# Doing segment 1's layer norm in the opening of a fused attention and GLU kernel

## The chip, the cores and the metric

The kernel runs on one core of a Trainium2 chip. The metric is device time in microseconds (us), the median of a few executions; a lower time is better. The engines are called as the profile calls them: PE is TensorE (PEld its weight loads), DVE is VectorE, ACT is ScalarE, POOL is GpSimd, and SP is SyncE, whose queue issues nearly all transfers here.

## The reference

One adaptive-norm block with segmented attention, followed by a bilinear GLU. All arrays are float32, there are 2048 tokens of width 512, 32 heads of 16, and 4 segments of 512 tokens.

```python
h = _layernorm(x) * (1 + ca) + sa            # norm of every token, scaled and shifted per column
for s in range(4):                           # segments of 512 tokens, q/k/v of h
    logits = q_s @ k_s.T * scale + mask      # causal inside the segment
    a_dot  = softmax(logits) @ v_s
    a_mem  = (phi(q_s) @ M) / (phi(q_s) @ z + 1e-6)      # memory of the earlier segments
    o_s    = g * a_mem + (1 - g) * a_dot
    M, z   = M + phi(k_s).T @ v_s, z + sum(phi(k_s))     # phi(t) = t + 1 if t > 0 else exp(t)
x = x + ga * (o @ wo)
x = x + gb * ((h2 @ w_gate) * (h2 @ w_up) @ w_down)      # h2: second norm, with cb and sb
```

The vectors sa, ca, ga, sb, cb and gb come from `silu(c) @ w_mod`.

## The kernel before

**Attention part.** A segment's norm (`ln`, through `a_ln`) reads four tiles of x (128 tokens by 512). For each tile VectorE takes statistics (a bn_stats and a bn_aggr). Then two ACT instructions (Ln, Exp) and a few four-element operations, on VectorE for segment 0 and on POOL for the others, give 1/sqrt(var+eps). Four tensor_scalar instructions on VectorE normalise the tiles. After that the tiles are transposed on PE and scaled, shifted and split in two parts (`ahH`, `ahL`) by ACT and POOL. Keys and queries are made per group g of 8 heads (`a_kq`): 12 matmuls into a PSUM bank (`kps`, `qps`), a copy `kf`/`qf` on ACT, and a split in three bfloat16 parts, for groups 1 to 3 with ACT and POOL (`k`, `kr` on lines 823 to 828 for keys, the same for queries). They are written to DRAM (`kd`, `qd`) and read back in a different layout as `kst` and `qst`. The features phi of the keys are made by ACT and finished by a scalar_tensor_tensor on VectorE (`phk`).

**The loop over units.** A unit is half a group: four heads of one segment. For each there are passes of PE: `q` tiles (queries by keys), whose row maxima VectorE takes straight from PSUM in a custom instruction (line 39, out `q`, and the maxima in `nm`), and `k` tiles (keys by queries), whose exponentials ACT writes to `pt`. The q tiles live in two PSUM banks, `lq0` and `lq1`, used in turn: PE can write the next q tile into a bank only after VectorE is through with the one before. Between these tiles PE gets other work ("fill"): keys, queries and values of later groups and segments, memories, the output projection. Before the loop stands the opening: modulation vectors, segment 0's norm, keys and queries of groups 0 and 1, and `gates`, which makes `omg` and `gg` from beta with a few VectorE instructions, copies `omg` into eight value tiles on POOL (line 683) and scales the head mask `hmg` with both.

**What sets the order.** PE's instructions are chained in program order by `pe`. `CV` and `CA` chain the VectorE and ACT instructions issued through them in the same way; instructions issued through `vec` or `act` join that chain only when those are switched to it, which is done for `vec` just before the loop (`vec.eng = CV`). The rest is placed by a list scheduler at build time, so each engine has a fixed order at run time. Before the change, segment 1's norm is woven into segment 0's groups 2 and 3 inside the loop, nine steps in all: four pairs of statistics, the small operations, four normalisations. Its x goes into the four buffers `x`, which before that hold segment 0's x and then the raw weights `wk` and `wq` of groups 1 and 2 (the list `stage`).

Of the kernel before, what the change touches and what calls it, by code (L numbers as in the profile page):

```python
# [8 lines left out]
F32 = mybir.dt.float32  # L9
F32R = mybir.dt.float32r  # L10
BF = mybir.dt.bfloat16
AF = mybir.ActivationFunctionType
# [5 lines left out]
P = 128  # L18
# [39 lines left out]
def tile_kernel(ctx, tc, x, wq, wk_, wv, wo, beta, w_gate, w_up, w_down, c, w_mod, out):  # L58
# [113 lines left out]
    def ln(pool, hpool, xt, s, sc, sh, pfx, hb, fast):  # L172

        first = pfx == "a" and s == 0
        V, A = (CV, CA) if first else (vec, act)
        mv = pool.tile([P, 4, 2], F32, tag="mv", name=f"{pfx}mv{s}", bufs=2)
        for t in range(4):
            st = pool.tile([P, 6], F32, tag="st", name=f"{pfx}st{s}_{t}", bufs=2)
            i = V.bn_stats(st, xt[t])
            if not first:  # L180
                pin(i)
            V.bn_aggr(mv[:, t, :], st)
            if not first:
                yield 0.0
        sd = pool.tile([P, 4], F32, tag="sd", name=f"{pfx}sd{s}", bufs=2)
        A.activation(sd, mv[:, :, 1], AF.Ln, bias=epst[:, 0:1])
        y = pool.tile([P, 4], F32, tag="y", name=f"{pfx}y{s}", bufs=2)
        A.activation(y, sd, AF.Exp, scale=-0.5)
        a = pool.tile([P, 4], F32, tag="ya", name=f"{pfx}ya{s}", bufs=2)
        b = pool.tile([P, 4], F32, tag="yb", name=f"{pfx}yb{s}", bufs=2)  # L190
        eng = CV if first else nc.gpsimd
        eng.tensor_mul(a, y, y)
        if first:
            CV.scalar_tensor_tensor(b, mv[:, :, 1], EPS, a, op0=ALU.add, op1=ALU.mult)
        else:
            eng.tensor_scalar(b, mv[:, :, 1], 1.0, EPS, op0=ALU.mult, op1=ALU.add)
            eng.tensor_mul(b, b, a)
        eng.tensor_scalar(b, b, -0.5, 1.5, op0=ALU.mult, op1=ALU.add)
        eng.tensor_mul(y, y, b)
        yield 0.0  # L200
        tps = [bank(f"{pfx}tp{s}_{d}") for d in range(KT)] if first else []
        for t in range(4):
            i = V.tensor_scalar(xt[t], xt[t], mv[:, t, 0:1], y[:, t:t + 1],
                                op0=ALU.subtract, op1=ALU.mult)
            if not first:
                pin(i)
                yield 0.0
            for d, ps in enumerate(tps):
                TP(ps[:, t * P:(t + 1) * P], xt[t][:, d * P:(d + 1) * P], ident)
        if first:  # L210
            yield 0.0
        hH, hL = [], []
        if first:
            hcur[0] = hH, hL
        for d in range(KT):
            if first:
                ps = tps[d]
            else:
                ps = bank(f"{pfx}tp{s}_{d}", small=pfx == "c" and s == 0)
                for t in range(4):  # L220
                    TP(ps[:, t * P:(t + 1) * P], xt[t][:, d * P:(d + 1) * P], ident)
            h = pool.tile([P, L], F32, tag="hf", name=f"{pfx}hf{s}_{d}", bufs=hb[2])
            A.activation(h, ps, AF.Identity, scale=sc[:, d:d + 1], bias=sh[:, d:d + 1])
            hi = hpool.tile([P, L], F32R, tag=hb[0].format(d), name=f"{pfx}hH{s}_{d}", bufs=hb[1])
            lo = hpool.tile([P, L], F32R, tag=hb[0].format(4 + d), name=f"{pfx}hL{s}_{d}", bufs=hb[1])
            if fast:
                if d % 2:
                    A.activation(hi, h, AF.Copy)
                else:
                    V.tensor_copy(hi, h)  # L230
                V.tensor_sub(lo, h, hi.bitcast(F32))
            else:
                act.activation(hi, h, AF.Copy)
                nc.gpsimd.tensor_sub(lo, h, hi.bitcast(F32))
            hH.append(hi)
            hL.append(lo)
            yield 0.45
            if pfx == "a" and not first and d % 2 == 1:
                yield False
        return hH, hL  # L240
# [500 lines left out]
                i += 1  # L741

    wH, wL = {}, {}
    stage = [("ph", 3), ("ph", 3), ("ph", 3), ("mem", 1), ("pkr", 1), ("f", 2)] + [("x", 4)] * 4 + [("mem", 1), ("memb", 2)]
    nst = [0]

    def staged(nm):
        tg, n = stage[nst[0] % len(stage)]
        nst[0] += 1
        return (ap if tg == "memb" else pa).tile([P, D], F32, tag=tg, name=f"wr{nm}", bufs=n)  # L750

    def load_g(nm, w, g):
# [46 lines left out]
    def a_kq(s, g, nm):  # L799

        hH, hL = hcur[0]
        ph = phs.setdefault((s, g), {})
        if True:
            dst = kd if nm == "k" else qd
            ps = bank(f"{nm}ps{s}_{g}")
            n = 0
            three = ((wH, hH), (wH, hL), (wL, hH)) if s == 0 and g < 2 else ((wH, hH), (wL, hH), (wH, hL))
            terms = [(k, *ab) for k in range(KT) for ab in three]
            if s == 0 and g == 1:
                terms.sort(key=lambda t: t[1] is wL)  # L810
            for k, a, b in terms:
                MM(ps, a[nm, g][:, k, :], b[k], start=n == 0, stop=n == 11)
                n += 1
                if n in (3, 6, 9):
                    yield 0.68
            f = pa.tile([P, L], F32, tag="f", name=f"{nm}f{s}_{g}", bufs=2)
            fast = s == 0 and g == 0
            A, V = (CA, CV) if fast else (act, nc.gpsimd)
            A.activation(f, ps, AF.Copy)
            q3 = pa.tile([P, 3, L], BF, tag="q3", name=f"{nm}3_{s}_{g}", bufs=2)  # L820
            r = pa.tile([P, L], F32, tag="qr", name=f"{nm}r_{s}_{g}", bufs=2)
            i0, i1, i2 = (0, 1, 2) if nm == "k" else (2, 1, 0)
            A.activation(q3[:, i0, :], f, AF.Copy)
            V.tensor_sub(r, f, q3[:, i0, :])

            def rest():
                (CV.tensor_copy if fast else act.copy)(q3[:, i1, :], r)
                V.tensor_sub(q3[:, i2, :], r, q3[:, i1, :])
                nc.sync.dma_start(dst[s][g].rearrange("r p t -> p r t"), q3)

            if fast:
                rest()
            phi = (nm == "k" and s < NSEG - 1) or (nm == "q" and s > 0)
            if phi:
                if fast:
                    yield 0.0
                if nm == "q" and g > 0:
                    yield from drain()
                e = pa.tile([P, L], F32, tag="ph", name=f"ph{nm}{s}_{g}", bufs=3)
                if behind or after:  # L840
                    settle()
                rl = pa.tile([P, L], F32, tag="rl", name=f"rl{nm}{s}_{g}", bufs=1)
                ph[nm] = e

                def feature():
                    for a, fn in ((rl, AF.Relu), (e, AF.Exp)):
                        i = (CA if fast else act).activation(a, f, fn)
                        if lastex[0] is not None:
                            tc.add_manual_dep(i.ins, lastex[0].ins.name, NOSYNC, reason="order")

                def feature2():
                    pin((CV if fast else vec).scalar_tensor_tensor(e, e, 1.0, rl, op0=ALU.min, op1=ALU.add))

                held = s > 0 or g > 1
                if held:
                    behind.append(lambda: (feature(), after.append(feature2)))
                else:
                    feature()
            yield 0.68
            if not fast:  # L860
                rest()
            if phi and not held:
                later.append(feature2)
                if fast:
                    flush()
        nkq[s, g] = nkq.get((s, g), 0) + 1
        if nkq[s, g] == 2:
            done.add((s, g))
# [107 lines left out]
    def fill_a():  # L976
# [1 line left out]
            next(w)  # L978
        yield from av
        memq.extend((a_mem(0, 0), a_mem(0, 1)))  # L980
        lns = None
        for s in range(NSEG):
            if s > 0:
                hcur[0] = yield from lns
# [2 lines left out]
            for g in range(2 if s == 0 else 0, NG):  # L987
# [5 lines left out]
                K, Q = a_kq(s, g, "k"), a_kq(s, g, "q")  # L993
                if s == NSEG - 1 and g == 0:
                    B["orl"] = wo_load(0, wpool)
                if g >= 2 and s + 1 < NSEG:
                    if g == 2:
                        xts[s + 1] = xload(s + 1)
                        lns = a_ln(s + 1)
                        Q = weave(Q, lns, (0, 1, 2, 3))  # L1000
                    else:
                        K = weave(K, lns, (1,) if s > 0 else (0, 1, 3))
                        Q = weave(Q, lns, (0, 1, 2, 3) if s > 0 else (0, 1))
                if g == 1 and 0 < s < 3:
                    acc = mod_acc(r)
                    K, Q = weave(K, acc, (0, 2)), weave(Q, acc, (0, 2))
# [120 lines left out]
    w1 = [load_g(nm, w, 1) for nm, w in (("k", wk_), ("q", wq))]  # L1127
    for w in w1:
        next(w)
    run(kq0[1])  # L1130
    run(kq0[0])
    load(0)
# [4 lines left out]
        next(w)  # L1137
    for i in range(3):
        next(av)
    gates()  # L1140
    w2 = [load_g(nm, w, 2) for nm, w in (("k", wk_), ("q", wq))]
    for w in w2:
# [536 lines left out]
```

## Time and profile before

| | |
|---|---|
| median of 3 runs | 854.42 us (854.02 to 854.63) |
| the profiled execution's own time | 853.83 us |
| span of the profiled execution | 852.1 us |
| PE busy | 835.4 us (98%) |
| DVE busy | 641.9 us (75%) |
| ACT busy | 498.0 us (58%) |
| POOL busy | 275.7 us (32%) |

The span runs from the first to the last instruction; 1.7 us of the execution's own time lie around it. Timeline rows give the start in the span, the duration in us, the engine, the line, the operation with output and inputs, the count of merged instructions, and in brackets the idle time of the engine just before with what ended it. Window rows give busy time and count of each engine in a stretch of time.

### The profile page before, as it was taken

The numbers are of one execution on the slowest core, as the hardware profiler recorded it, in microseconds if no ns is written. First come the engines' busy times: TensorE is split into PE (matmuls) and PEld (weight loads), VectorE is DVE, ScalarE is ACT, GpSimd is POOL, SyncE is SP. The second block draws the span as 40 slices with busy tenths as digits, with TensorE's granted clock in tenths as the row PEclk, the third lists the DMA queues.
The fourth block names the chain that finished last, engine by engine and source line by source line (L and its number), as shares of the span: only waits on it lengthen the run. The fifth ranks groups of instructions, "written<-read, shape, count | busy, mean of one in ns | idle before, by whom it ended". The sixth has DMA issues, their size and how long they took to land.

```text
span 852.1 us, 14420 instructions
## 1 busy us (share of the span) xinstructions
PE 835.4 (98%) x4982; PEld 598.2 (70%) x4982; DVE 641.9 (75%) x1796; ACT 498.0 (58%) x759; POOL 275.7 (32%) x423
## 2 busy tenths in 40 slices
PE   9989999999999999999999999999999999999998
PEld 6756656666665656656665687887888778888886
DVE  7897868887778967787888359989987855447654
ACT  4758767787676876677545626344435546455230
POOL 2756627566565774675424610000000000000000
PEclk9999999999999999999999999999999999999999
DMA  9655445564545554457675457587650675335102
GB/s 272 153 150 158 111 114 136 164 171 120 144 103 166 146 163 106 123 155 230 173 233 161 137 193 238 187 286 273 233 220 28 234 269 211 123 135 185 42 9 98
DMA packets 83928, 139.57 MB, mean 164 GB/s; under 512 B 12720, under 2 KB 46768, under 8 KB 83856
## 3 DMA queue, kind: packets, MB, share of 16 engines
q1 hardware_dynamic: 83568, 138.52, 52.6%
q8 instruction: 39, 0.64, 0.3%
q14 instruction: 33, 0.27, 0.1%
q10 hardware_dynamic: 288, 0.15, 0.1%
HBM read 89.87 MB, written 48.50 MB: 162 GB/s over the span
## 4 chain that ended last, share of the span: by engine, by line
PE 60%; DVE 4%; ACT 2%; POOL 2%; issue 1%; DMA 0%; DVEq 0%; POOLq 0%; ACTq 0%
PE acc L1355 14%; PE Xu L1286 7%; PE Xg L1286 7%; PE wops L85 5%; PE tb L85 4%; PE Yu L1286 4%; PE Yg L1286 4%; PE k L85 3%; PE q L85 3%; DVE q L39 2%; PE Zg L1286 1%; PE Zu L1286 1%; PE qps L85 1%; PE vps L85 1%; PE ctp L88 1%; PE Xx L1286 1%
## 5 line engine op out<-in xcount | busy, mean ns | idle before, releaser
L39 DVE CUSTOM_DVE_ANT_0 q<-q,cmask 128x384 f32<-128x384 f32 (+3 forms) x512 | 248.3, 503 | 72.2 <-PE q L85 64.6
L335 ACT ACTIVATE pt<-k 128x1024 f32<-128x1024 f32 x160 | 163.9, 1024 | 74.2 <-PE k L85 72.2
L341 POOL TENSOR_SCALAR_AFFINE_SELECT pt<-pt 128x256 f32<-128x256 f32 (+1 forms) x224 | 97.6, 449 | 137.9 <-ACT pt L335 135.9
L85 PE MATMUL q<-kst,qst 96*128 96x384 bf16 (+3 forms) x512 | 122.8, 302 | 6.4 <-DVE nm L39 5.1
L85 PE MATMUL k<-qst,kst 98*128 98x384 bf16 (+3 forms) x512 | 96.0, 299 | 1.6 <-ACT pt L335 1.3
L1363 DVE TENSOR_TENSOR xa<-xa,acc 128x512 f32<-128x512 f32 x95 | 64.9, 684 | 39.1 <-PE acc L1355 38.5
L85 PEld LDWEIGHTS <-qst 96*128 96x128 bf16 x512 | 43.9, 98 | 57.8 <-issue 43.0
L85 PE MATMUL tb<-pt,v 128*32 128x512 f32 (+3 forms) x1024 | 75.7, 436 | 0.3 <-POOL pt L341 0.3
L39 DVE DVE_READ_ACCUMULATOR2_ANT nm<- 128x1 f32 x512 | 72.0, 141 | 0.0
L85 PEld LDWEIGHTS <-kst 98*128 98x128 bf16 x512 | 44.5, 98 | 25.0 <-issue 8.8
L1355 PE MATMUL acc<-dH,mH 128*128 128x512 f32 (+1 forms) x152 | 60.3, 397 | 0.0
L1355 PE MATMUL acc<-dL,mH 128*128 128x512 f32 (+1 forms) x152 | 60.1, 395 | 0.0
L1355 PE MATMUL acc<-dH,mL 128*128 128x512 f32 (+1 forms) x152 | 60.0, 395 | 0.0
L85 PEld LDWEIGHTS tb<-pt,v 128*32 128x32 f32 x1024 | 28.6, 109 | 39.2 <-issue 35.5
L367 ACT ACTIVATE tsb<-tb 128x512 f32<-128x512 f32 x32 | 19.1, 596 | 31.7 <-PE tb L85 31.6
L1355 PEld LDWEIGHTS acc<-dL,mH 128*128 128x128 f32 (+1 forms) x152 | 28.6, 188 | 7.1
L1355 PEld LDWEIGHTS acc<-dH,mL 128*128 128x128 f32 (+1 forms) x152 | 28.5, 188 | 7.1 <-DVE mL L1306 0.3
L1355 PEld LDWEIGHTS acc<-dH,mH 128*128 128x128 f32 (+1 forms) x152 | 28.5, 188 | 6.7
L85 PE MATMUL kps<-ahH,wkH 128*128 128x512 f32 x64 | 29.5, 460 | 0.0
L85 PE MATMUL qps<-ahH,wqH 128*128 128x512 f32 x64 | 28.7, 449 | 0.0
L85 PE MATMUL wops<-woH,oH 128*128 128x512 f32 x64 | 28.3, 442 | 0.0
L85 PE MATMUL vps<-wvH,ahH 128*128 128x512 f32 x64 | 28.3, 442 | 0.0
(399 smaller groups left out, 2018.4 us busy)
## 6 DMA issues: line engine op xcount, KB each, us to landing
wm<-in_w_mod_dram SPq DMA_DIRECT2D x24, 256.0 KB, 4.6
kd<-k SPq DMA_DIRECT2D x16, 384.0 KB, 2.5
qd<-q SPq DMA_DIRECT2D x16, 384.0 KB, 3.3
kst<-kd SPq DMA_DIRECT2D x32, 192.0 KB, 3.3
qst<-qd SPq DMA_DIRECT2D x32, 192.0 KB, 3.8
x<-in_x_dram SPq DMA_DIRECT2D x16, 256.0 KB, 4.7
kst<-kd SPq DMA_DIRECT2D x32, 128.0 KB, 3.2
qst<-qd SPq DMA_DIRECT2D x32, 128.0 KB, 3.8
```

The source lines that it names most:

```text
L39: i = getattr(self.eng, name)(*a, **k)
L85: return pe(nc.tensor.matmul(*a, **k))
L88: return pe(nc.tensor.transpose(*a))
L335: ex = act.activation(pt, kp, AF.Exp, scale=0.25)
L341: sels[u, i] = nc.gpsimd.affine_select(w, w, pattern=[[0, w.shape[1]], [1, P]], compare_op=ALU.is_ge, fill=0.0, base=0, channel_multiplier=-1)
L367: act.activation(tsbs[u], tbs.pop(u), AF.Copy)
L1286: pe(nc.tensor.matmul(ps[0:n], a, b[:, k], start=first and c == 0, stop=last and c == 5, skip_group_check=True))
L1355: pe(nc.tensor.matmul(ps, a[0:m, t * P:(t + 1) * P], b[0:m], start=j == 0, stop=j == n - 1))
L1363: vec.tensor_add(xa, xa, ps)
```

## The change

The nine steps of segment 1's norm are run in the opening, behind the first two value tiles and ahead of `gates`. Its x is loaded behind the weights of group 1 and ahead of those of group 2. `vec` is switched to the chain `CV` before that. For segment 1 the Ln and Exp go into ACT's chain and the small operations go from POOL to VectorE, with one instruction fewer. The copy `kf`/`qf` of group 1 joins ACT's chain too. Since the `x` buffers are taken, the raw weights of groups 1 and 2 are staged in buffers of `pt`. The transposes and what follows stay where they were.

```diff
@@ ln
-        A.activation(sd, mv[:, :, 1], AF.Ln, bias=epst[:, 0:1])
+        E = CA if s < 2 else act
+        E.activation(sd, mv[:, :, 1], AF.Ln, bias=epst[:, 0:1])
...
-        A.activation(y, sd, AF.Exp, scale=-0.5)
+        E.activation(y, sd, AF.Exp, scale=-0.5)
...
-        eng = CV if first else nc.gpsimd
+        eng = CV if s < 2 else nc.gpsimd
         eng.tensor_mul(a, y, y)
-        if first:
+        if s < 2:
             CV.scalar_tensor_tensor(b, mv[:, :, 1], EPS, a, op0=ALU.add, op1=ALU.mult)
...
-    stage = [("ph", 3), ("ph", 3), ("ph", 3), ("mem", 1), ("pkr", 1), ("f", 2)] + [("x", 4)] * 4 + [("mem", 1), ("memb", 2)]
+    stage = [("ph", 3), ("ph", 3), ("ph", 3), ("mem", 1), ("pkr", 1), ("f", 2)] + [("pt", PT)] * 4 + [("mem", 1), ("memb", 2)]
...
@@ a_kq
-            A.activation(f, ps, AF.Copy)
+            (CA if s == 0 and g < 2 else act).activation(f, ps, AF.Copy)
...
@@ fill_a
-        lns = None
+        lns = ln1
...
-                if g >= 2 and s + 1 < NSEG:
+                if g >= 2 and 0 < s < NSEG - 1:
...
-                        K = weave(K, lns, (1,) if s > 0 else (0, 1, 3))
-                        Q = weave(Q, lns, (0, 1, 2, 3) if s > 0 else (0, 1))
+                        K = weave(K, lns, (1,))
+                        Q = weave(Q, lns, (0, 1, 2, 3))
...
@@ the opening
     for w in w1:
         next(w)
+    xts[1] = xload(1)
     run(kq0[1])
     run(kq0[0])
     load(0)
...
     for i in range(3):
         next(av)
+    vec.eng = CV
+    ln1 = a_ln(1)
+    for _ in range(9):
+        next(ln1)
     gates()
```

The order of PE's instructions is the same before and after, row for row. On DVE the first place is the end of the opening, from the last part of group 0's queries to the first q tile of the loop. Before:

```order
L39 SCALAR_TENSOR_TENSOR phk_0_451<-phk_0_451,rlk_0_452 128x512
L39 TENSOR_SCALAR omg<-omg 128x32
L39 TENSOR_SCALAR gg<-gg 128x32
L39 RECIPROCAL gg<-gg 128x32
L39 RECIPROCAL omg<-omg 128x32
L852 SCALAR_TENSOR_TENSOR phk_1_543<-phk_1_543,rlk_1_544 128x512
L39 ISA q_0_0_594,nm_593<-q_0_0_594,cmask 128x512
```

After, behind the same `phk_0` and three of the four statistics pairs (ast into amv), which aren't shown:

```order
L39 BN_STATS ast_3_512<-x_3_445 128x6
L39 BN_AGGR amv_502<-ast_3_512 128x2
L39 TENSOR_TENSOR aya_519<-ay_517 128x4
L39 SCALAR_TENSOR_TENSOR ayb_520<-amv_502,aya_519 128x4
L39 TENSOR_SCALAR ayb_520<-ayb_520 128x4
L39 TENSOR_TENSOR ay_517<-ay_517,ayb_520 128x4
L39 TENSOR_SCALAR x_0_439<-x_0_439,amv_502,ay_517 128x512
L39 TENSOR_SCALAR x_1_441<-x_1_441,amv_502,ay_517 128x512
L39 TENSOR_SCALAR x_2_443<-x_2_443,amv_502,ay_517 128x512
L39 TENSOR_SCALAR x_3_445<-x_3_445,amv_502,ay_517 128x512
L39 TENSOR_SCALAR omg<-omg 128x32
```

All 16 instructions of the norm (eight of statistics, four small ones, four normalisations) now stand between `phk_0` and `omg`, so ahead of `gates`, of `phk_1` and of the loop's first q tile; the rows `gg`, the two reciprocals, `phk_1` and the first q tile follow as before.

The second place is POOL in the same stretch, from the low parts of group 1's weights (the first wkL, wqL) over those of group 2 to group 1's keys and queries. Before:

```order
L764 TENSOR_TENSOR wqL_437<-wrq_435,wqH_436 128x4x8x16
L683 COPY v_0_162<-omg 128x32
L683 COPY v_1_163<-omg 128x32
L683 COPY v_2_164<-omg 128x32
L683 COPY v_3_165<-omg 128x32
L683 COPY v_0_166<-omg 128x32
L683 COPY v_1_167<-omg 128x32
L683 COPY v_2_168<-omg 128x32
L683 COPY v_3_169<-omg 128x32
L688 TENSOR_TENSOR hmg<-hmg,gg 128x8x16 x4
L764 TENSOR_TENSOR wkL_518<-wrk_516,wkH_517 128x4x8x16
L764 TENSOR_TENSOR wqL_522<-wrq_520,wqH_521 128x4x8x16
```

After:

```order
L767 TENSOR_TENSOR wqL_437<-wrq_435,wqH_436 128x4x8x16
L767 TENSOR_TENSOR wkL_553<-wrk_551,wkH_552 128x4x8x16
L767 TENSOR_TENSOR wqL_557<-wrq_555,wqH_556 128x4x8x16
L827 TENSOR_TENSOR kr_1_575<-kf_1_572,k_0_1_574 128x512
L684 COPY v_0_162<-omg 128x32
L684 COPY v_1_163<-omg 128x32
L684 COPY v_2_164<-omg 128x32
L684 COPY v_3_165<-omg 128x32
L684 COPY v_0_166<-omg 128x32
L684 COPY v_1_167<-omg 128x32
L684 COPY v_2_168<-omg 128x32
L684 COPY v_3_169<-omg 128x32
```

The low parts of group 2's weights and the residual `kr` of group 1's keys now stand ahead of the copies of `omg`; behind the copies come group 1's `k`, the first `hmg` rows, `qr`, the other `hmg` rows and `q`. On ACT, Ln, Exp and the Exp for `gg` stand between group 2's `wqH` and group 1's `kf`. Inside the loop the statistics and normalisations are gone from DVE, with nothing in their place: before, two statistics pairs stood between the q tiles q_2_0 and q_2_1 of the second unit, one pair between its q_3_0 and q_3_1, and the rest further down.

More of the change, by code (lines that the diff above doesn't have):

```diff
@@ L749, in staged @@
         nst[0] += 1
+        if tg == "pt":
+            return ap.tile([P, 2, 512], F32, tag=tg, name=f"wr{nm}", bufs=n)[:, 0]
         return (ap if tg == "memb" else pa).tile([P, D], F32, tag=tg, name=f"wr{nm}", bufs=n)
```

## The prediction

> **What bounds the kernel now.** First the page's busy times, then busy time by stretches around the place of the change.
>
> ```profile
> PE 835.4 (98%) x4982; PEld 598.2 (70%) x4982; DVE 641.9 (75%) x1796; ACT 498.0 (58%) x759; POOL 275.7 (32%) x423
> 37.00:50.00 13.00, 11.71 (x64) 7.93 (x62) 11.72 (x45) 6.11 (x9) 8.66 (x10) 1.00 0.68 188
> 50.00:60.00 10.00, 8.46 (x48) 5.57 (x48) 9.69 (x36) 6.29 (x11) 5.62 (x6) 1.00 0.52 149
> 60.00:76.00 16.00, 15.75 (x116) 10.28 (x116) 14.31 (x54) 11.90 (x19) 7.27 (x17) 1.00 0.28 83
> 76.00:80.00 4.00, 3.25 (x25) 2.18 (x23) 3.69 (x14) 4.00 (x7) 4.00 (x5) 1.00 0.90 203
> 80.00:140.00 60.00, 59.94 (x444) 37.47 (x441) 43.09 (x161) 44.54 (x64) 31.00 (x46) 1.00 0.47 124
> ```
>
> Columns of a stretch: length, then busy time of PE, PEld, DVE, ACT and POOL, the granted clock, DMA share, GB/s. PE is the bound; a change of the order on other engines can only add to or take from its idle time, 16.7 us in the whole span (852.1 - 835.4). From 37 to 80 us PE idles 3.83 us (1.29 + 1.54 + 0.25 + 0.75), and from 80 to 140 us 0.06 us. So an earlier or later PE at 80 us stays so: nothing behind absorbs it. From 50 to 60 us DVE is 97% busy; from 76 to 80 us ACT and POOL are full instead.
>
> **What leaves the loop.** The timeline of DVE and that of PE where the norm stands now:
>
> ```profile
> 51.27 0.69 DVE L39 BATCH_NORM_STATS2 ast<-x 128x6 f32<-128x512 f32 x1
> 52.89 0.67 DVE L39 CUSTOM_DVE_ANT_0 q<-q,cmask 128x512 f32<-128x512 f32 x1
> 54.95 0.69 DVE L39 BATCH_NORM_STATS2 ast<-x 128x6 f32<-128x512 f32 x1
> 55.77 0.54 DVE L39 CUSTOM_DVE_ANT_0 q<-q,cmask 128x384 f32<-128x384 f32 x1
> 53.67 0.38 PE L85 MATMUL q<-kst,qst 96*128 96x384 bf16 x2 [0.42 <-DVE nm L39]
> 55.14 0.38 PE L85 MATMUL q<-kst,qst 96*128 96x256 bf16 x2 [0.66 <-DVE nm L39]
> 56.81 0.38 PE L85 MATMUL q<-kst,qst 96*128 96x256 bf16 x2 [0.36 <-DVE nm L39]
> 62.23 0.38 PE L85 MATMUL q<-kst,qst 96*128 96x512 bf16 x1 [0.15 <-DVE nm L39]
> ```
>
> Two statistics pairs hold up the q maxima by 1.62 us (51.27 to 52.89), a third by 0.82 (54.95 to 55.77), and behind them PE waits for DVE to hand back a PSUM bank: 0.42 + 0.66 + 0.36 + 0.15 = 1.59 us. With the pairs gone DVE is ahead by more than each of these waits, so I take all four as saved: **-1.6 us**. The fourth pair and the four normalisations stand further on, where PE hardly waits (0.25 us from 60 to 76), so they bring next to nothing. Bounds: at least 1.0, since PE's next q tile can then be held by an exponential on ACT; at most 2.5, all of PE's idle time from 50 to 80 (1.54 + 0.25 + 0.75). What is late next is ACT, from 76 us on. POOL's five small operations and ACT's Ln and Exp leave stretches in which those engines have gaps: nothing.
>
> **What the norm costs in the opening.** The same 16 instructions ran for segment 0 with POOL out of the way:
>
> ```profile
> 5.22 0.69 DVE L39 BATCH_NORM_STATS2 ast<-x 128x6 f32<-128x512 f32 x1 [0.48 <-DMA x<-in_x_dram]
> 8.34 0.18 DVE L39 BATCH_NORM_AGGREGATE amv<-ast 128x2 f32<-128x6 f32 x1
> 9.12 0.16 DVE L39 TENSOR_TENSOR aya<-ay 128x4 f32<-128x4 f32 x1 [0.60 <-ACT ay L39]
> 9.92 1.92 DVE L39 TENSOR_SCALAR x<-x,amv,ay 128x512 f32<-128x512 f32 x4
> ```
>
> Statistics 3.30 us (5.22 to 8.52), 0.60 until ACT has done Ln and Exp, 0.80 for the four small ones, 1.92 for the normalisations: 6.62 us. At its new place DVE is not so free, and POOL is busy:
>
> ```profile
> 27.12 2.19 DVE L39 SCALAR_TENSOR_TENSOR phk<-phk,rlk 128x512 f32<-128x512 f32 x1
> 29.23 1.65 DVE L39 TENSOR_SCALAR omg<-omg 128x32 f32<-128x32 f32 x1
> 32.27 0.35 DVE L39 RECIPROCAL omg<-omg 128x32 f32<-128x32 f32 x1 [0.91 <-POOL v L683]
> 33.71 3.76 DVE L852 SCALAR_TENSOR_TENSOR phk<-phk,rlk 128x512 f32<-128x512 f32 x1 [1.08 <-ACT phk L847]
> 37.39 0.69 DVE L39 CUSTOM_DVE_ANT_0 q<-q,cmask 128x512 f32<-128x512 f32 x1
> 53.48 0.69 DVE L39 SCALAR_TENSOR_TENSOR phk<-phk,rlk 128x512 f32<-128x512 f32 x1
> 28.72 2.13 POOL L764 TENSOR_TENSOR wqL<-wrq,wqH 128x512 fp32r<-128x512 f32 x1
> 30.95 1.29 POOL L683 COPY v<-omg 128x32 f32<-128x32 f32 x8
> 32.17 1.49 POOL L688 TENSOR_TENSOR hmg<-hmg,gg 128x128 f32<-128x128 f32 x4
> 33.61 1.70 POOL L764 TENSOR_TENSOR wkL<-wrk,wkH 128x512 fp32r<-128x512 f32 x1
> 35.17 1.69 POOL L764 TENSOR_TENSOR wqL<-wrq,wqH 128x512 fp32r<-128x512 f32 x1
> 37.81 1.33 POOL L824 TENSOR_TENSOR kr<-kf,k 128x512 f32<-128x512 f32 x1
> 30.02 1.27 ACT L763 ACTIVATE wqH<-wrq 128x512 fp32r<-128x512 f32 x1
> 32.01 0.63 ACT L823 ACTIVATE k<-kf 128x512 bf16<-128x512 f32 x1
> ```
>
> The scalar_tensor_tensor for `phk` takes 0.69 us in the loop, but 2.19 and 3.76 us here, beside POOL's long tensor_tensor rows; even `omg`, 32 elements, takes 1.65 us and ends just as POOL's wqL does (30.88 against 30.85). So certain DVE operations (tensor_scalar from SBUF, two-input operations) stand still until POOL ends an instruction. Statistics don't: I take them at 0.82 a pair.
>
> With that, DVE's schedule after, step by step. `phk_0` ends at 29.31 as before. Statistics: to 32.6. ACT (whose wqH ends at 31.29, so it waits here now) does Ln and Exp: 33.2. POOL now follows wqL (to 30.85) by group 2's pair, 1.55 each (33.61, 35.17, 36.72 before): busy to 33.95, and the first small operation waits for that; the four end at 34.75. Meanwhile ACT, 2 us late, does the Exp for `gg`, then `kf` and `k` (0.6 + 0.63) to 34.6, and POOL takes `kr` (1.33) to 36.0 ahead of the normalisations: they end at 37.9. Had they gone first, `kr` would have ended there and the copies of `omg` behind it begun at the same time. `omg` 0.2, POOL's copies 1.29, the reciprocal of `omg`, which must wait for these copies, 0.35: 39.75. POOL has begun `k` (1.33) at 39.4, so `phk_1` stands until 40.7 and ends at 41.4, where it ended at 37.47 before. **+3.9 us** until DVE takes the first q tile. Bounds: without any stop by POOL 29.31 + 6.62 + 0.2 + 1.29 + 0.1 + 0.35 + 0.69 = 38.56, +1.1; with `phk_1` held through POOL's next rows too, `hmg` x4 (1.49), 42.9, +5.4.
>
> `phk_1` of before, ready at 33.71, was passed over when POOL changed from wkL to wqL at 35.2, and got in at 36.78 only; passed over once more here it would cost one `hmg` row (1.49 / 4 = 0.4). [...]
>
> **Does it reach PE?** PE's order is unchanged:
>
> ```profile
> 36.03 0.39 PE L85 MATMUL q<-kst,qst 96*128 96x512 bf16 x1
> 37.66 0.91 PE L85 MATMUL q<-kst,qst 96*128 96x512 bf16 x3
> ```
>
> The first q tile goes to bank `lq0`, the next to `lq1` (37.66), and the third, in the same row, needs `lq0` back: DVE finished with it at 38.08, hardly later than PE came. Behind it in PE's queue stand value matmuls that need nothing from DVE, but they can't pass. So PE stops at about 37.9 for DVE's whole delay, and PE and DVE go on from there in the old pattern, both later. Nothing covers it.
>
> **Loads and queues.** On SP, x of segment 1 now stands where group 2's weights stood, and these follow behind. Landing times in that stretch, and ACT's first use of the weights:
>
> ```profile
> wrk<-in_wk_dram SPq DMA_DIRECT2D x2, 256.0 KB, 7.4
> wrq<-in_wq_dram SPq DMA_DIRECT2D x2, 256.0 KB, 7.5
> 15.21 0.51 SPq L758 DMA_DIRECT2D wrq<-in_wq_dram  x1
> 29.02 1.26 ACT L763 ACTIVATE wkH<-wrk 128x512 fp32r<-128x512 f32 x1
> ```
>
> Four x loads issued from 14 to 17 land by 24.5 even at 7.5 us; statistics begin at 29.3. Group 2's weights, issued by about 18.5, land by 26, for 29.02. Nothing. Group 3's weights move behind `kd` of group 1, to about 41; that is in time, since ACT uses them at about 49 by then.
>
> **Sum.** +3.9 - 1.6 = **+2.3 us**. The profiled execution would go from its own 853.83 to 856.1; the median shown is 0.6 higher, 854.42, so I forecast 856.7 us.
>
> **Rivals.**
> 1. *The norm finds its room in DVE's gaps, and the kernel gets faster.* Place: DVE between 27 and 37 us, where it sat idle 0.91 + 1.08 us and stood still 1.5 + 1.5 + 3.1 us beside POOL: 8.1 us, more than the norm's 6.62. If POOL's rows fall into the norm's pauses instead of stopping it, the cost is the lower bound 1.1, against a saving up to 2.5: -1.4 us, 853.0, and a little less if PE's waits before 50 us ease too. It decides for faster when DVE takes its first q tile before 39 us. Against it: `phk_1` comes after the copies of `omg`, and POOL has `k` ready just then.
> 2. *PE runs slower after its stop.* At the start of the span PE had been idle. From 3 to 5 us only 6 of its 512-column matmuls fall in the stretch, from 6 to 8 us 11 (the last few a little smaller), both at a granted clock of 1.00 in the row:
>
> ```profile
> 3.00:5.00 2.00, 2.00 (x6) 0.70 (x5) 0.51 (x3) 0.43 (x2) 0.13 (x1) 1.00 0.73 204
> 6.00:8.00 2.00, 2.00 (x11) 0.78 (x8) 1.93 (x6) 0.00 (x0) 2.00 (x3) 1.00 1.06 377
> ```
>
> So a PE that comes from idling works at about half the rate for some us. The longest of the four PE waits above is 0.66 us; a stop of 3.9 could bring that state back, for 3 to 4 us at half rate: +1.7 on top, 858.4. [...]
> 3. *The change doesn't do what it says: x comes too late*, after 29.3, and the whole chain waits. It would take a landing of over 12 us, and each us costs one: 857.7 for one.
>
> **How the numbers follow.** About 0.2% (1.7 us) is what a measurement of this kernel can tell from no change. The forecast's case, POOL stopping DVE (net +0.5 to +3.7), 0.60: slower 0.45, within 0.15. Rival 1 (net -1.4 to +0.5, or a little below), 0.25: faster 0.12, within 0.13. Rival 2, 0.10: slower. Rival 3, 0.05: slower. Sum: faster 0.12, within 0.28, slower 0.60. Range: from net -0.8 (into rival 1) to +4.7 (upper end 5.4 - 1.0 = 4.4, and some of rival 2): 853.6 to 859.1.
>
> **What would show it.** Right: DVE's first q tile at 40.5 to 42 us; one PE wait for DVE of 3 to 4.5 us at 38; tensor_scalar x rows in the opening longer than 0.55 each or with gaps between; `phk_1` again far over 0.69; the waits of 1.59 us behind 50 us gone. Wrong: a first q tile before 39.5; a PE wait below 2 us; PE's waits between 50 and 64 (in the old count) still there; or a difference that arises after 80 us, where I expect none.

## The result and the profile after

The changed kernel takes **857.66 us** (median of 7 runs, 855.27 to 859.01), the kernel before 854.42 us beside it (7 runs, 853.9 to 854.84): ratio 1.0035, 95% interval 1.0025 to 1.0045, so 3.2 us slower. The execution that was profiled is the quickest of the seven, 855.27 us with a mean granted clock of 0.999; the other six have 0.995 to 0.998 and 856.8 to 859.01 us. The runs of before have 0.999 to 1.000. That difference turns out to matter, so this profile shows what the change does when the clock holds.

The page's busy times and the same stretches as before (length, then PE, PEld, DVE, ACT, POOL, granted clock, DMA share, GB/s):

```profile
PE 834.6 (98%) x4982; PEld 597.7 (70%) x4982; DVE 640.6 (75%) x1800; ACT 497.9 (58%) x759; POOL 275.1 (32%) x418
...
37.00:50.00 13.00, 8.72 (x47) 5.83 (x46) 10.76 (x38) 3.83 (x6) 7.53 (x20) 1.00 0.35 102
50.00:60.00 10.00, 9.53 (x57) 6.58 (x55) 9.25 (x38) 6.43 (x11) 6.63 (x6) 1.00 0.42 112
60.00:76.00 16.00, 16.00 (x119) 10.37 (x118) 12.72 (x49) 11.74 (x17) 7.67 (x14) 1.00 0.39 106
76.00:80.00 4.00, 3.47 (x28) 2.62 (x26) 3.61 (x15) 4.00 (x7) 3.10 (x5) 1.00 0.80 185
```

PE's idle time from 37 to 50 us went from 1.29 to 4.28 us (13.00 - 8.72); from 50 to 76 it went from 1.79 to 0.47. Roughly, the first is the price and the second the gain. The timeline of PE around both:

```profile
37.71 0.39 PE L85 MATMUL q<-kst,qst 96*128 96x512 bf16 x1
41.41 0.38 PE L85 MATMUL q<-kst,qst 96*128 96x384 bf16 x2 [3.31 <-DVE nm L39]
...
57.43 0.38 PE L85 MATMUL q<-kst,qst 96*128 96x256 bf16 x2 [0.29 <-DVE nm L39]
...
77.78 0.60 PE L85 MATMUL k<-qst,kst 98*128 98x256 bf16 x4 [0.38 <-ACT pt L336]
```

One stop of 3.31 us at 38, where PE of before idles 0.14 us. Of the waits of before behind 50 us one is left, of 0.29 us. The wait for ACT at 76.80 grew from 0.20 to 0.38. DVE and POOL in the opening:

```profile
29.28 0.68 DVE L39 BATCH_NORM_STATS2 ast<-x 128x6 f32<-128x512 f32 x1
...
33.16 1.05 DVE L39 TENSOR_TENSOR aya<-ay 128x4 f32<-128x4 f32 x1 [0.60 <-ACT ay L39]
...
34.64 1.02 DVE L39 TENSOR_TENSOR ay<-ay,ayb 128x4 f32<-128x4 f32 x1
35.70 1.92 DVE L39 TENSOR_SCALAR x<-x,amv,ay 128x512 f32<-128x512 f32 x4
...
39.09 0.35 DVE L39 RECIPROCAL omg<-omg 128x32 f32<-128x32 f32 x1 [0.91 <-POOL v L684]
39.36 1.33 DVE L39 SCALAR_TENSOR_TENSOR phk<-phk,rlk 128x512 f32<-128x512 f32 x1
40.61 0.68 DVE L39 CUSTOM_DVE_ANT_0 q<-q,cmask 128x512 f32<-128x512 f32 x1
```
```profile
32.51 1.68 POOL L767 TENSOR_TENSOR wqL<-wrq,wqH 128x512 fp32r<-128x512 f32 x1
34.47 1.17 POOL L827 TENSOR_TENSOR kr<-kf,k 128x512 f32<-128x512 f32 x1 [0.28 <-ACT k L826]
37.77 1.29 POOL L684 COPY v<-omg 128x32 f32<-128x32 f32 x8 [2.12 <-DVE omg L39]
38.99 1.15 POOL L831 TENSOR_TENSOR k<-kr,k 128x512 bf16<-128x512 f32 x1
```

DVE's first q tile starts at 40.61 instead of 37.39: 3.22 us late. `aya`, four elements a partition, took 1.05 us instead of 0.16 and ended with POOL's `wqL` (34.21 and 34.19); `ay` took 1.02 and ended with `kr` (35.66 and 35.64); `phk_1` took 1.33 instead of 0.69, across POOL's `k`. The statistics, beside POOL's long rows too, took the 0.66 to 0.69 us that they take in the loop.

PE's rows stand in the same order in all these kernels, but for the 14 that experiment 2 adds, so each can be paired with its row of before. How much later it starts, in us, worked out so for this kernel and the experiments below:

```
row of before       after   e1    e2    e3    e4    e5    e6    e7    e8    e9    e10
37.66 q             0.05   1.13 -0.04 -0.05  0.02  0.36  0.48  0.07  0.10  0.11  0.68
38.38 vps           3.22   4.60  3.21  3.46  2.02  0.40  0.47  0.02  1.37  0.10  4.74
43.20 kps           3.24   6.90  3.22  4.97  2.02  0.41  0.48  0.01  1.39  0.10  6.76
52.85 qps           3.23   6.90  3.23  4.95  2.02  0.41  0.49  0.00  1.38  0.11  6.74
55.36 mz            2.29   5.96  2.30  4.95  2.01  0.39 -0.45 -0.94  1.40 -0.83  5.81
57.03 k             1.77   5.44  1.77  4.95  2.01  0.40 -0.97 -0.63  1.39 -1.35  5.28
62.68 kps           1.20   4.98  1.29  4.95  2.00  0.39 -1.08 -0.05  1.39 -1.77  5.02
64.96 mp            0.98   4.76  1.07  4.96  2.02  0.39 -1.31 -0.28  1.40 -2.01  4.80
94.65 tb            0.99   4.78  1.08  4.97  2.03  0.40 -1.30 -0.26  1.41 -2.00  4.81
349.92 q            1.03   4.80  1.12  4.95  2.07  0.38 -1.33 -0.22  1.43 -1.99  4.85
599.97 acc          1.27   5.74  0.31  4.81  3.19  1.11 -0.36  0.30  2.25 -1.19  5.82
```

After: +3.2 at one place, -2.24 in six steps between 52.85 and 64.96, then nothing up to 350 us. So with the clock held the change costs about +1.0 us there; the median says +3.2.

Between the last two rows of the table the executions part again, by -0.8 to +1.1 us. After, e1 and e2 run the same instructions there and move by +0.2, +0.9 and -0.8, so this belongs to the single execution, and the lags are read up to 350 us only.

### The profile page after: what moved, and what is told of

The parts are those of the page before. It is cut to its first block, busy times and chain, and to the rows that moved or that the text cites. A ratio compares the mean times of both kernels' runs of the same rounds, so it can differ in the third digit from the quotient of the medians.

```text
span 853.5 us, 14430 instructions
## 1 busy us (share of the span) xinstructions
PE 834.6 (98%) x4982; PEld 597.7 (70%) x4982; DVE 640.6 (75%) x1800; ACT 497.9 (58%) x759; POOL 275.1 (32%) x418
## 4 chain that ended last, share of the span: by engine, by line
PE 58%; DVE 5%; ACT 2%; POOL 2%; DMA 1%; issue 1%; SPq 0%; DVEq 0%; ACTq 0%; POOLq 0%
PE acc L1363 14%; PE Xg L1294 6%; PE Xu L1294 6%; PE wops L85 5%; PE tb L85 4%; PE Yu L1294 4%; PE Yg L1294 4%; PE k L85 3%; PE q L85 3%; DVE q L39 2%; PE Zg L1294 1%; PE Zu L1294 1%; PE qps L85 1%; PE vps L85 1%; PE Xx L1294 1%
## 5 line engine op out<-in xcount | busy, mean ns | idle before, releaser
L1371 DVE TENSOR_TENSOR xa<-xa,acc 128x512 f32<-128x512 f32 x95 | 64.8, 683 | 39.2 <-PE acc L1363 37.4
```

Source lines behind the costliest of these rows:

```text
L1371: vec.tensor_add(xa, xa, ps)
```

## The experiments

**1. The changed kernel again (e1_again).** No edit.

> The changed kernel once more, nothing edited, for a profile of one of its slower executions. The profiled execution of after took 855.27 us, 1.4 over its counterpart of before, and the other six 856.8 to 859.0 at a mean granted clock of 0.995 to 0.998. Theory 1 (stop of PE alone): a stop of 3.3 us at 38 us, 1.6 to 1.7 regained by 60 us, so +1.5 to +1.7 whatever the execution, and the rest is noise that shows nowhere in particular. Theory 2 (the stop also lowers PE's clock): in a slower execution the granted clock falls below 1.00 in the us right behind 40, matmul rows there get about twice as long, and the span is longer by about half of that stretch; times spread from +1.4 to +4.6 with the mean clock. Rival theory 3 (loads): the slower executions wait longer for a transfer somewhere.

Median 858.58 us (857.72 to 859.57, 5 runs), ratio 1.0047 (1.0035 to 1.0059), clocks 0.995 to 0.997. The profiled execution was the longest, 859.57. Its stretches of 1 us behind the stop, and its PE rows:

```profile
40.00:41.00 1.00, 0.00 (x0) 0.00 (x0) 0.68 (x2) 0.00 (x0) 1.00 (x3) 1.00 0.00 0
41.00:42.00 1.00, 0.00 (x0) 0.00 (x0) 1.00 (x2) 0.00 (x0) 1.00 (x2) 0.62 0.00 0
...
44.00:45.00 1.00, 1.00 (x4) 0.81 (x3) 0.28 (x2) 0.58 (x1) 1.00 (x5) 0.50 1.10 312
...
47.00:48.00 1.00, 1.00 (x4) 0.81 (x3) 0.97 (x5) 0.00 (x0) 0.00 (x0) 0.50 0.79 272
48.00:49.00 1.00, 1.00 (x6) 0.55 (x5) 0.05 (x1) 0.60 (x1) 0.00 (x0) 0.97 0.35 121
```
```profile
38.79 0.39 PE L85 MATMUL q<-kst,qst 96*128 96x512 bf16 x1
42.64 0.58 PE L85 MATMUL q<-kst,qst 96*128 96x384 bf16 x2 [3.46 <-DVE nm L39]
...
43.98 0.63 PE L85 MATMUL vps<-wvL,ahH 128*128 128x512 f32 x1
44.41 0.63 PE L85 MATMUL vps<-wvH,ahH 128*128 128x512 f32 x1
...
49.39 0.40 PE L85 MATMUL kps<-ahH,wkL 128*128 128x512 f32 x1
49.63 0.40 PE L85 MATMUL kps<-ahL,wkH 128*128 128x512 f32 x1
```

PE goes idle at 39.2; the clock falls at about 41.2 (a mean of 0.62 from 41 to 42), still inside the stop, and is 0.50 until 48. Matmuls of 512 columns start 0.43 us apart there (43.98, 44.41) and 0.24 behind it (49.39, 49.63). DVE's first q tile is 4.45 us later than in before (41.84, quoted below, against 37.39), PE at the end of the half clock 6.90 (table): **2.4 us** lost there. (The 1.13 in the table's first row is a wait of PE for ACT's copy `qf`, 0.47 us at 37.98; e10 has one of 0.24 at 37.53.) This is the prediction's second rival, and eleven of the twelve runs of the changed kernel so far have a mean clock below 0.999. PE had been idle for 2.1 us when the clock fell, and stood for 1.4 us more.

The same execution shows why the first term varies. DVE's `phk_0`, ahead of the norm, and POOL:

```profile
27.52 3.85 DVE L39 SCALAR_TENSOR_TENSOR phk<-phk,rlk 128x512 f32<-128x512 f32 x1
...
35.97 2.88 DVE L39 TENSOR_SCALAR x<-x,amv,ay 128x512 f32<-128x512 f32 x4
...
41.84 0.69 DVE L39 CUSTOM_DVE_ANT_0 q<-q,cmask 128x512 f32<-128x512 f32 x1
```
```profile
29.09 1.73 POOL L767 TENSOR_TENSOR wqL<-wrq,wqH 128x512 fp32r<-128x512 f32 x1
30.76 2.16 POOL L767 TENSOR_TENSOR wkL<-wrk,wkH 128x512 fp32r<-128x512 f32 x1
```

Here `phk_0` was passed over when POOL began wqL, and waited for that row too (3.85 us; 2.19 in the first execution). The norm began 2 us later, but its small operations then met no POOL row, and only the normalisations did (2.88 instead of 1.92, across POOL's `kr`, 1.17 us from 36.49). Net: DVE's delay was 4.1 us (4.45, less the 0.4 by which this execution was late already) instead of 3.2.

**2. Work for PE in the stop (e2_fill).** If the clock is the missing part, useless matmuls in the stop must bring it back, though DVE comes as late as ever.

```diff
+    vec.memset(gab, 0.0)
...
+            if v == -2 and slot == 3:
+                wf = psp.tile([P, 2, 512], F32, tag="lk", name="wf", bufs=1)
+                wz = gab.bitcast(BF)[:, 0:512]
+                for _ in range(14):
+                    MM(wf[:, 0], wz[:, 0:P], wz, start=True, stop=True)
```

> The changed kernel with 14 unused 512-column matmuls (0.22 us each, 3.0 us) ahead of the third q tile, where PE stops for 3.3 us. The stop stays (PE can only go on when VectorE does), but PE is busy in it. Theory 1: same time as the changed kernel, about 857.5. Theory 2: the clock stays at 1.00 in every execution and the time is 855.0 to 856.0 with a small spread, +0.6 to +1.6 over before. Theory 3: as theory 1.

855.0 us (853.87 to 855.66, 11 runs), ratio 1.0003 (0.9994 to 1.0011), every clock 0.999 to 1.000.

```profile
37.85 3.19 PE L85 MATMUL wf<-gab 128*128 128x512 bf16 x14
41.40 0.38 PE L85 MATMUL q<-kst,qst 96*128 96x384 bf16 x2 [0.36 <-DVE nm L39]
```

PE's own row waits as long (3.21 in the table) and the lag at the end is 1.08, as in the first profile. What differs is the clock: 857.66 and 858.58 against 855.0, 2.7 to 3.6 us of the medians. So the half clock behind the stop is the larger part of the loss, and the stop, net of what the loop saves, the smaller: e2 lies 0.35 us above before beside it (854.65) by the medians, with an interval from -0.5 to +0.9.

**3. The stop by itself, in three lengths (e3_stop3, e4_stop2, e8_stop1).** Into the kernel before, useless statistics on DVE ahead of the loop, 7, 5 and 4 of them; the last 5, 3 and 2 stand behind `phk_1`. The norm stays in the loop. I had put such an instruction at 0.62 us; it took 0.70 to 0.72, so the stops are longer than planned.

```diff
+    vec.memset(gab, 0.0)
...
+    for _ in range(7):
+        pin(CV.bn_stats(gbb[:, 0:6], gab))
```

> The kernel before with seven statistics instructions of no use on VectorE, two ahead of phk_1 (where VectorE waits anyway) and five behind it, ahead of the first q tile: 5 x 0.62 = 3.1 us. Norm and loads as before. Theory 1: PE stops for 3.1 us, nothing is regained: +3.1, 857.5. Theory 2: the same plus 1 to 3 us in most executions, 858.5 to 860.5, with the mean clock below 0.999 in them. Theory 3: 857.5, clock 1.000.

> The same with five statistics instructions, three of them behind phk_1: 3 x 0.62 = 1.9 us. Theory 1 and 3: +1.9, 856.3. Theory 2 with a threshold: a stop of 1.9 us is too short to lower the clock, so +1.9, mean clock 1.000 and a spread as small as that of before; if the clock falls here too, the threshold is below 2 us.

> The kernel before with four statistics instructions of no use, two of them behind phk_1: a stop of PE of 1.3 us. Where does the clock's threshold lie? If it falls only after a longer stop: 855.9 to 856.1, clock 1.000 in every execution. If any stop of more than a us or so can do it: some executions at 857 to 858 with a clock of 0.998, fewer than the four of six at 1.9 us.

DVE's statistics and the PE row that waits for them, of the longest, then the middle one, then the shortest:

```profile
37.35 3.60 DVE L39 BATCH_NORM_STATS2 gbb<-gab 128x6 f32<-128x512 f32 x5
...
41.66 0.38 PE L85 MATMUL q<-kst,qst 96*128 96x384 bf16 x2 [3.65 <-DVE nm L39]
...
43.00:44.00 1.00, 1.00 (x6) 0.35 (x5) 0.16 (x2) 0.00 (x0) 0.00 (x0) 0.53 0.83 197
...
46.00:47.00 1.00, 1.00 (x5) 0.49 (x5) 0.00 (x0) 0.52 (x1) 0.00 (x0) 0.77 0.98 336
```
```profile
40.21 0.38 PE L85 MATMUL q<-kst,qst 96*128 96x384 bf16 x2 [2.14 <-DVE nm L39]
...
42.00:44.00 2.00, 2.00 (x11) 1.31 (x9) 1.63 (x6) 0.60 (x1) 0.45 (x1) 1.00 0.86 222
```
```profile
37.44 1.41 DVE L39 BATCH_NORM_STATS2 gbb<-gab 128x6 f32<-128x512 f32 x2
...
39.56 0.38 PE L85 MATMUL q<-kst,qst 96*128 96x384 bf16 x2 [1.41 <-DVE nm L39]
```

- Stop of 3.65 us: 860.52 us (858.64 to 861.22, 5 runs), ratio 1.0065 (1.0053 to 1.0077), clocks 0.995 to 0.998. The profiled execution, its best, loses 3.5 at the stop and 1.5 more at a clock of 0.50. There the clock fell at about 43.1 us (a mean of 0.53 from 43 to 44), when PE had been at work again since 41.66, and rose at about 46.5.
- Stop of 2.14 us: 858.94 us (856.12 to 859.85, 6 runs), ratio 1.0047 (1.0035 to 1.006). Two executions with a mean clock of 1.000 took 857.02 and 856.12; four with 0.998 took 858.86 to 859.85. I had expected this one too short to lower the clock; in four of six it wasn't, and those cost some 2.5 us more.
- Stop of 1.41 us: 856.01 us (854.44 to 856.75, 11 runs), ratio 1.0016 (1.0007 to 1.0025), every clock 0.999 to 1.000.

In the table, e4 and e8 keep their 2.0 and 1.4 us up to 350 us: a late start of DVE at 37.4 is paid in full and never made up, as the prediction had it. And of these three stops, that of 1.41 us lowered the clock in none of eleven executions, that of 2.14 in four of six, and that of 3.65 in all five.

**4. The loads alone (e5_loads).** From before: `xts[1] = xload(1)` behind group 1's weights, and the staging in `pt` tiles, with DVE, ACT, POOL and PE as they were.

```diff
-                        xts[s + 1] = xload(s + 1)
+                        if s > 0:
+                            xts[s + 1] = xload(s + 1)
...
+    xts[1] = xload(1)
```

> The kernel before with the change's transfers and buffers alone: x of segment 1 loaded behind group 1's weights, the raw weights staged in pt; the norm stays in the loop. My theory: nothing, 854.3 to 855.0, and the loop's q tiles at the times of before within 0.1 us. Rival (the early x and the later weights of group 2 hold somebody up): up to 1 us more.

854.58 us (854.42 to 855.63, 10 runs), ratio 1.0004 (0.9995 to 1.0013): nothing. The 0.4 us in the table are there from the first rows on, from the 20 warm-up matmuls, which are the same in both kernels (before, then this one):

```profile
1.69 6.53 PE L85 MATMUL wups<-wu 128*128 128x512 bf16 x20 [1.69 <-DVE wu L650]
```
```profile
1.69 7.17 PE L85 MATMUL wups<-wu 128*128 128x512 bf16 x20 [1.69 <-DVE wu L650]
```

So an offset that stands in the first row of the table is the execution's, not the edit's, and is to be taken off.

**5. No norm for segment 1 at all (e6_no_norm).** From after: statistics, the four small operations, Ln and Exp, and the normalisations are left out for segment 1, whose x goes on unnormalised. It was meant to bound what any better place can bring.

```diff
+        skip = pfx == "a" and s == 1
-        for t in range(4):
+        for t in range(0 if skip else 4):
```

> The changed kernel without the norm of segment 1 (its 16 VectorE instructions and ACT's Ln and Exp are left out, x goes to the transposes as it is), so neither the loop nor the opening pays for it. This measures what taking the norm out of the loop is worth by itself. My theory after the first four runs: 2.2 us at the loop's 80th q instruction (the changed kernel went from 3.2 behind to 1.0 behind), of which 1.7 by its 28th: 852.4. By the sum in the prediction: 1.6, 853.0. The mean clock stays at 1.000.

852.8 us (851.61 to 853.5, 10 runs), ratio 0.9979 (0.997 to 0.9988). From the table, 0.48 to -1.31: 1.8 us. That is less than the 2.24 of the changed kernel, because PE stops here once more for DVE at 57.1 (0.44 us), where the changed kernel does not; I did not follow that up. It is less than e9 gains below, too, so it bounds nothing.

**6. The whole norm behind the gates (e10_norm_behind_gates).** From after: the block of the nine norm steps is moved from ahead of `gates()` to behind it, so that POOL's copies don't wait for the norm.

```diff
+    gates()
     vec.eng = CV
     ln1 = a_ln(1)
...
-    gates()
```

> The whole norm in the opening, but behind gates instead of ahead of them: POOL's order stays as in the kernel before. Theory: VectorE's free 4.2 us (32.6 to 36.8) take that much of the norm's 6.6, and phk_1 follows: first q tile 2.4 to 3.2 us late, a stop of PE of 2.3 to 3.1, some 2.2 regained, +0.2 to +1.0 without the clock. The clock falls in most executions, since 1.9 us was enough in four of six: 856.0 to 858.0, mean clock 0.996 to 0.998 in the slower ones. Rival (the place ahead of gates was the trouble, with POOL's copies queued behind it): first q tile at most 1.5 us late, clock 1.000, below 854.4.

859.46 us (858.48 to 859.66, 5 runs), ratio 1.0053 (1.0039 to 1.0067), slower than I had said, with clocks of 0.995 to 0.997. DVE, POOL and PE:

```profile
37.75 2.76 DVE L39 TENSOR_SCALAR x<-x,amv,ay 128x512 f32<-128x512 f32 x4
40.43 1.64 DVE L39 SCALAR_TENSOR_TENSOR phk<-phk,rlk 128x512 f32<-128x512 f32 x1
41.99 0.69 DVE L39 CUSTOM_DVE_ANT_0 q<-q,cmask 128x512 f32<-128x512 f32 x1
...
38.57 1.20 POOL L827 TENSOR_TENSOR kr<-kf,k 128x512 f32<-128x512 f32 x1 [0.92 <-ACT k L826]
...
42.78 0.48 PE L85 MATMUL q<-kst,qst 96*128 96x384 bf16 x1 [4.05 <-DVE nm L39]
```

The normalisations met `kr` (2.76 us instead of 1.92, beside its 1.20), and the stop was longer, not shorter. Neither of the two places tried for the whole norm escapes POOL; other orders were not run.

**7. Only the statistics in the opening (e7_stats_behind_gates, e9_stats_only).** What runs unhindered beside POOL is the statistics (0.66 to 0.68 us in the changed kernel's opening, 0.66 to 0.69 in the loop of before); what PE waited for behind 50 us was the statistics too. So, from the loads alone, the four statistics steps go behind `gates()`, into DVE's wait ahead of `phk_1`, and the rest stays in the loop: in e7 moved up into the statistics' old places, in e9 where before has it.

```diff
+    vec.eng = CV
+    ln1 = a_ln(1)
+    for _ in range(4):
+        next(ln1)
...
-                        lns = a_ln(s + 1)
+                        lns = ln1 if s == 0 else a_ln(s + 1)
-                        Q = weave(Q, lns, (0, 1, 2, 3))
+                        Q = weave(Q, lns, (0, 1, 2, 3) if s > 0 else ())
```

(e9; e7 keeps that last line as it was, and thins out the later weaves for segment 1 instead, to one step.)

> Only the four statistics pairs in the opening, behind the VectorE instructions of gates and ahead of phk_1; Ln, Exp, POOL's small operations and the normalisations stay in the loop. VectorE idled or stood still for POOL from 32.6 to 36.8 us there, and statistics run beside POOL. Theory (the stop is the cost, and it comes from where the norm was put): phk_1 still ends at about 37.4, the first q tile is at most 0.3 us late, PE doesn't stop, the clock stays, and 1.4 to 1.6 of the loop's waits are saved: 852.8 to 853.4, faster than both kernels. Rival (any statistics there push phk_1 past one more instruction of POOL): first q tile 1 to 1.5 us late, 854 to 855.

> As the run with the statistics behind gates, but the four normalisations stay at the loop places that they have in the kernel before (there they had moved up into the statistics' places, and 0.3 of the 0.9 us saved by the 24th q instruction was gone by the 28th). Theory: first q tile on time, 1.5 us ahead of before by the 28th q instruction, and at most 1.0 left behind 80 us, since ACT is full there: 853.4 to 854.0, clock 1.000. Rival (ACT takes nearly all of it back, as in that run): 854.2 to 854.7.

e7: 854.71 us (853.97 to 855.35, 11 runs), ratio 1.0004 (0.9995 to 1.0013), not the gain that I had forecast. DVE and PE of e7:

```profile
54.01 1.19 DVE L39 TENSOR_SCALAR x<-x,amv,ay 128x512 f32<-128x512 f32 x1
58.62 1.47 DVE L39 TENSOR_SCALAR x<-x,amv,ay 128x512 f32<-128x512 f32 x1
...
56.18 0.38 PE L85 MATMUL q<-kst,qst 96*128 96x256 bf16 x2 [0.67 <-DVE nm L39]
62.17 0.38 PE L85 MATMUL q<-kst,qst 96*128 96x512 bf16 x1 [0.56 <-DVE nm L39]
```

The opening was free (0.02 in the table), and 0.94 us were won by the row at 55.36; but two of the four normalisations, put where the statistics had stood, took 1.19 and 1.47 us instead of 0.55, and PE waited 0.67 and 0.56 us again behind them.

e9: **852.63 us** (852.24 to 852.9, 9 runs), ratio 0.9976 (0.9966 to 0.9986), 2.1 us below the median of before beside it (854.73) and better than I had said; clocks 0.999 to 1.000. DVE and PE of e9:

```profile
35.78 1.78 DVE L39 SCALAR_TENSOR_TENSOR phk<-phk,rlk 128x512 f32<-128x512 f32 x1
37.49 0.69 DVE L39 CUSTOM_DVE_ANT_0 q<-q,cmask 128x512 f32<-128x512 f32 x1
...
54.32 0.38 PE L85 MATMUL q<-kst,qst 96*128 96x256 bf16 x2 [0.29 <-DVE nm L39]
```

`phk_1` of before stood from 33.71 to 37.47 for POOL's sake; the statistics fill that time, and `phk_1` ends when it did, so the first q tile moves 0.1 us. The whole gain of the changed kernel behind 50 us is there (0.11 to -2.01), without its price. It beats both kernels.

## Why the prediction was right, and where it wasn't

856.7 us was forecast, 857.66 measured, inside the range, and slower as said. The mechanism named is the one that the profile shows, but two of the terms were off by 1.3 us together, more than the +1.0 that they leave, and a rival held too cheap makes up most of the median's difference.

- **DVE's first q tile late, +3.9.** Measured +3.2 in the first profiled execution and +4.1 in the second; POOL's rows stop DVE as said, and the bounds of 1.1 to 5.4 held both. In the first, the term was over-sized step by step: the normalisations ended at 37.6 (37.9 forecast), the reciprocal of `omg` at 39.4 (39.75), `phk_1` at 40.7 (41.4), because POOL's `kr` and `k` took 1.17 and 1.15 us, not 1.33, and `k` began earlier. In the second `phk_0` itself was passed over, which no step of the forecast had.
- **It reaches PE whole, and nothing behind absorbs it.** Right: one stop of 3.31 us at 38, and in e3, e4 and e8 the lag stays up to 350 us.
- **-1.6 saved in the loop.** Measured -2.24. The four waits did go, but for 0.29 us of the second. The term was short because a wait by the profile is not all that PE loses: at 0.42, 0.36 and 0.15 PE's later rows move by 0.59, 0.52 and 0.32, 0.16 to 0.17 more each, and two gaps for which no wait is shown gave 0.22 each. The last matmul ahead of a gap is drawn with its full 0.38 to 0.40 us where the next would start 0.23 after it. The upper bound of 2.5 held.
- **What is late next is ACT.** Right, but small: the wait at 76.80 grew by 0.18 us, and no more of the saving was lost there.
- **Loads and queues: nothing.** Right (e5).
- **Rival 2, half clock behind the stop, chance 0.10, +1.7.** This was the usual case: eleven of twelve runs, and 2.7 to 3.6 us by the medians with the stop filled. The chance was too low, and no run stood behind it: in e1 the clock fell 2.1 us after PE had stopped, and a stop of 2.14 us was enough in four of six executions of e4. No run shows the +1.7 from 3 to 4 us at half rate either, which was my estimate: the half clock lasted 6.8 us in e1 and 3.4 in e3 (last section), and cost 2.4 and 1.5 there. The row of before that I leaned on, half-speed matmuls at the start (6 of them in 2 us, later 11), did point to the right state.
- **No difference behind 80 us.** Right up to 350 us (0.99 and 1.03); the scatter behind that is not the change's.
- **Rivals 1 and 3.** Neither came: DVE's first q tile was past 39 in both executions, and x was there in time.

The net of the two terms was +2.3 by the prediction and +1.0 by the profile; the missing 1.3 and another 0.9 came with the clock. That the total lay within 1 us is luck: an over-sized net stood in for a cost that the forecast's case left out. Counted by the traces: +3.2 to +4.1 for the stop, -2.2 in the loop, and 2.4 for the clock in the one trace of this kernel that shows it fall.

## What to carry to other kernels

Move the part of a chain that the waiting engine can do unhindered, not the chain: here the one-input statistics fitted into a stall that DVE had anyway (0.63 to 0.66 us each in e9), while beside POOL two of the small two-input operations took 1.05 and 1.02 us instead of 0.16, and the four normalisations 2.88 in e1 and 2.76 in e10 instead of 1.92, for a gain in the loop that e9 has without them (2.12 us of 2.24). A stop of PE was to be priced twice here, with its length and with the matmuls behind it (3.5 and 1.5 us in e3), and one of 2.14 us was long enough for that in four of six executions; so read the granted clock behind a stop in stretches of 1 us, and the mean clock of every run. Filling the stop with useless matmuls shows what the clock costs (2.7 to 3.6 us in e2). When one edit saves at one place and pays at another, pair the rows of the engine that bounds the kernel: the lag from row to row gives both, where the idle times alone are too small.

## What was not expected of the hardware

- The granted clock fell to 0.50 some 2 us after PE went idle in e1 (39.2 to 41.2 us), but 5 us after it in e3 (38.0 to 43.1), when PE had been back at work for 1.4. In e10 PE went idle at 38.7 and was at half rate when it came back at 42.78: matmuls of 512 columns start 0.43 us apart up to 47.56, and 0.23 from 47.83 on. A stop of 2.14 us lowered the clock in four executions of six, one of 1.41 us in none of eleven; the 3.31 us of the changed kernel's first profile left it at 1.00, the 3.46 of e1 did not.
- By the means of the stretches of 1 us, the half clock lasted 6.8 us in e1 (41.24 to 48.06) and 3.4 in e3 (43.06 to 46.46). What decides whether a stop lowers the clock, and for how long, no run set by itself.
- Which operation POOL's rows stop changes between executions of one kernel: `phk_0` took 2.19 us in one and 3.85 in another, with the norm 2 us later.
- The 20 warm-up matmuls took 6.38 us in the profiled execution of the changed kernel, 6.53 in that of before and 7.17 in that of e5, where all that follows up to 350 us starts 0.36 to 0.41 us later than in before.
